# Transposed output tiles of a gated mix: one DMA transpose per tile, narrower store pieces, one store semaphore

## The chip, the cores and the metric

The kernel runs on one core of a Trainium2 chip. The metric is the device time of one execution in microseconds. Ratios are the mean time of one kernel's runs over the mean of the runs of the kernel before in the same rounds; they are therefore not quite the ratio of the medians that are quoted beside them.

Names: PE is the matrix engine, DVE the vector engine, ACT the scalar engine, POOL the general engine (here, after a few small set-up operations, it only issues four loads), SP the engine whose queue issues nearly all DMAs, "SPq" in the profile. PEld is the loading of weights into PE.

## The reference, cut to what matters

```python
x = A_x                                        # 1 x 2048 x 640, bf16
g = sigmoid((x * gate_w).sum(-1, keepdims=True))
a = ssm(x)                                     # complex diagonal state space, 640 states, scan over 2048 steps
b = gelu(x @ w1 + b1) @ w2 + b2                # 640 -> 1728 -> 640
return g * a + (1 - g) * b
```

## The kernel before

The 2048 rows of x are handled as four tiles (`q` = 0 to 3) of 512 rows. Tiles 0 to 2 are computed transposed, with features on the partitions (`xT[q]`: 128 partitions x 5 feature blocks x 512 rows). DVE adds the parts of the result into `xT[q]`. Five DMA transposes, one for each feature block, then bring the tile back into row order, into a buffer `xn`, and one DMA stores it. Tile 3 is computed in row order chunk by chunk at the end and needs no transpose.

```python
xn = [SB(f"xn_{i}", [128, 4, D], BF16) for i in range(2)]        # two buffers, D = 640
# ...
# in outsT(q), q = 0, 1, 2:
op(f"o{q}", "dve", d_dve(2560, 2), K1, XT[q], lambda: tt(xf, xf, e1, ALU.add), prio=P)
load_T(f"oT{q}", f"l_oT{q}", [(xn[q % 2][:, :, d * 128:(d + 1) * 128], xT[q][:, d, :]) for d in range(KD)],   # KD = 5
       [("xn", q % 2, 0), ("xn", q % 2, 1)], 402 + q, 5.0, reads=XT[q])

def f_st():
    return dma_inc("sp", nc.sync.dma_start(o2[q * 512:(q + 1) * 512, :].rearrange("(c p) d -> p c d", p=128), xn[q % 2][:, :, :]), f"sto{q}")

op(f"sto{q}", "sp", 0.5, [("xn", q % 2, 0), ("xn", q % 2, 1)], [], f_st, prio=403 + q, lat=3.0)
```

`xn` has a second use: it holds the rows of x from which the gate is computed. POOL loads x of tile 2 into the first buffer and x of tile 3 into the second, so each of these loads has to wait until the store of tile 0 or tile 1 has read the buffer. Behind the load of tile 3 comes a chain: the gate product on DVE, a tanh on ACT, two small operations on DVE.

```python
def xnload(q, eng, prio=None):          # q = 2 and 3 are issued by POOL
    load(f"xn{q}", eng, f"l_xn{q}", xn[q % 2][:, :, :],
         x2[q * 512:(q + 1) * 512, :].rearrange("(c p) d -> p c d", p=128),
         [("xn", q % 2, 0), ("xn", q % 2, 1)], prio, dur=1.0, lat=6.0)
```

A list scheduler in the file fixes the order of instructions on each engine at build time.

## Time and profile before

The kernel before takes 213.39 us (median of 3; 212.97 to 213.45). Its profiled execution spans 213.0 us.

| Reading of the kernel before | Value | Where it is read |
|---|---|---|
| PE busy | 209.4 us, 98% | page, part 1 |
| DVE busy | 190.2 us, 89% | page, part 1 |
| From the start of steady matmuls to the last DVE operation | 14.63 to 210.29 us | chain that ended last |
| SP time to issue a tile's five transposes | 7.38, 7.00, 6.83 us | timeline of SP |
| Store of a tile, issue to landing | 6.3, 3.2, 3.2 us (tiles 0, 1, 2) | instructions of the store's line |
| Issue of the loads that reuse the buffers | 107.32, 156.99 us | timeline of POOL |

The page, part 1 (busy us, share of the span, number of instructions), of the kernel before:

```profile
PE 209.4 (98%) x1102; PEld 104.9 (49%) x1102; DVE 190.2 (89%) x240; ACT 103.2 (48%) x177; POOL 4.2 (2%) x12
```

The busy share alone does not prove that PE is the limit, since matmuls are pipelined. The Trainium skill has a pace to compare with: "TensorE: Matmul & The Clock Gate", section "Wait — 56ns, not 53.3ns?", says that warm back-to-back matmuls start N / 2.4 GHz + about 2.5 ns apart, 215.7 ns for N = 512. The chain below shows 65 such matmuls in 14.03 us, 215.8 ns each. This agrees within 0.1 ns, so in its steady part PE has nothing left to give at this number of matmuls.

The chain that ended last is what the profile finds when it starts from the last instruction and goes back, at each step, to what released it. In order of time (start us, duration us, what), of the kernel before:

```profile
14.63 5.40 PE ps L653 x25
...
144.85 14.03 PE ps L653 x65
158.88 14.06 PE ps L920 x78
...
204.80 5.47 PE ps L832 x50
210.27 0.02 issue
210.29 0.35 DVE W1sb L866
```

Every piece left out between 14.63 and 210.27 us is PE as well. No transpose, store or load of the output path stands in this chain.

The timeline of SP (start us, duration us of the issue, line, operation, what, how many) of the kernel before. L340 is the transpose, L992 the store of a tile:

```profile
91.79 7.38 SPq L340 DMA_TRANSPOSE xn<-xT  x5
100.40 0.38 SPq L992 DMA_DIRECT2D out_dram<-xn  x1
...
144.97 7.00 SPq L340 DMA_TRANSPOSE xn<-xT  x5
153.21 0.38 SPq L992 DMA_DIRECT2D out_dram<-xn  x1
...
192.65 6.83 SPq L340 DMA_TRANSPOSE xn<-xT  x5
```

The timeline of POOL, with the idle time before each load and what ended it in brackets:

```profile
107.32 0.77 POOL L333 DMA_DIRECT2D xn<-in_A_x_dram  x1 [64.08 <-DMA out_dram<-xn]
156.99 0.75 POOL L333 DMA_DIRECT2D xn<-in_A_x_dram  x1 [48.90 <-DMA out_dram<-xn]
```

These 113 us of waiting are the longest entry in the list of waits; POOL has no other work. What matters is when the reader of the loaded rows runs. It is DVE line 606, from 125.89 us for tile 2 and from 168.39 us for tile 3, without any wait before it.

### The profile page before, as it was taken

To read this page: it belongs to the slowest core of one execution; us is meant where nothing else is said; L and a number is where in the kernel's file an instruction comes from. 1 tells how busy PE (TensorE), PEld (TensorE's weight loads), DVE (VectorE), ACT (ScalarE), POOL (GpSimd) and SP (SyncE) were. 2 spreads that over 40 slices of the span, in tenths; PEclk is the share of its full clock that TensorE was granted. 3 is DMA by queue.
4 is the path that set the end of the run, shared out by engine and by line. 5 is a ranking of instruction groups with operands and counts; after the bars stand their busy time and mean duration, and the time that the engine had idled before them with its cause. 6 is when DMAs were issued, how large, how long until landed. Compare 5 with 4: busy or idle time off the path is not lost.

```text
span 213.0 us, 2755 instructions
## 1 busy us (share of the span) xinstructions
PE 209.4 (98%) x1102; PEld 104.9 (49%) x1102; DVE 190.2 (89%) x240; ACT 103.2 (48%) x177; POOL 4.2 (2%) x12
## 2 busy tenths in 40 slices
PE   8999999999999999999999999999999999999994
PEld 3444444444564444444464444444456444567774
DVE  2399999999999999999999999899999999499734
ACT  2389556679860353556680073456660037523330
POOL 1000000210000000000010000000010000000000
DMA  6999999999400020043474000005542000002531
GB/s 169 274 259 176 190 184 299 288 140 224 100 0 3 0 49 0 0 51 75 123 46 120 9 0 0 0 2 77 117 140 87 0 3 0 0 0 58 148 105 63
DMA packets 42664, 19.08 MB, mean 90 GB/s; under 512 B 34076, under 2 KB 41372, under 8 KB 42652
## 3 DMA queue, kind: packets, MB, share of 16 engines
q1 hardware_dynamic: 40992, 17.59, 37.6%
q0 software_dynamic: 1600, 1.32, 4.4%
q8 instruction: 8, 0.13, 0.3%
q14 instruction: 4, 0.03, 0.1%
q10 hardware_dynamic: 60, 0.01, 0.1%
HBM read 8.41 MB, written 2.63 MB: 52 GB/s over the span
## 4 chain that ended last, share of the span: by engine, by line
PE 97%; DMA 1%; DVE 0%; issue 0%
PE ps L653 22%; PE ps L696 20%; PE ps L920 20%; PE ps L967 15%; PE ps L783 7%; PE ps L832 5%; PE ps L631 5%; DMA xn<-in_A_x_dram 1%; PE ps L674 1%; PE ps L931 1%; PE ps L419 1%; PE ps L797 0%; DVE W1sb L866 0%; PE ps L438 0%
## 5 line engine op out<-in xcount | busy, mean ns | idle before, releaser
L653 PE MATMUL ps<-xT,W1sb 128*128 128x512 bf16 x220 | 48.1, 379 | 0.0
L736 DVE TENSOR_TENSOR_SCAN W<-atab,V 128x1280 bf16<-128x1280 f32 x16 | 44.3, 2812 | 0.3
L696 PE MATMUL ps<-xT,BT 128*128 128x512 bf16 x200 | 43.8, 379 | 0.0
L920 PE MATMUL ps<-Gl,W2sb 128*128 128x512 bf16 (+1 forms) x234 | 42.7, 344 | 0.0
L660 ACT ACTIVATE Gl<-ps,cols 128x512 bf16<-128x512 f32 x44 | 29.9, 694 | 15.5 <-PE ps L653 15.5
L653 PEld LDWEIGHTS ps<-xT,W1sb 128*128 128x128 bf16 x220 | 21.5, 98 | 26.0
L967 PE MATMUL ps<-Hb,CT 128*128 128x512 bf16 x150 | 32.9, 379 | 0.0
L920 PEld LDWEIGHTS ps<-Gl,W2sb 128*128 128x128 bf16 x234 | 22.9, 98 | 19.3
L705 ACT ACTIVATE U<-ps 128x512 bf16<-128x512 f32 x40 | 23.7, 596 | 15.6 <-PE ps L696 15.6
L696 PEld LDWEIGHTS ps<-xT,BT 128*128 128x128 bf16 x200 | 19.5, 98 | 23.8 <-ACT Gt L682 0.4
L938 ACT ACTIVATE E1T<-ps,cols 128x512 bf16<-128x512 f32 (+1 forms) x18 | 9.5, 624 | 36.0 <-PE ps L931 36.0
L967 PEld LDWEIGHTS ps<-Hb,CT 128*128 128x128 bf16 x150 | 14.5, 98 | 17.9 <-DVE Hb L488 0.3
L975 ACT ACTIVATE E2T<-ps 128x512 bf16<-128x512 f32 x15 | 9.1, 604 | 13.6 <-PE ps L967 13.6
L783 PE MATMUL ps<-W2sb,Gl 128*128 128x320 bf16 x104 | 14.8, 299 | 0.0
L606 DVE SCALAR_TENSOR_TENSOR trf<-xn,gwb 128x640 bf16<-128x640 bf16 x16 | 13.2, 823 | 0.4
L488 DVE TENSOR_TENSOR Hb<-Hb,V 128x1280 bf16<-128x1280 bf16 x16 | 12.5, 821 | 0.3
L488 DVE TENSOR_TENSOR V<-V,W 128x1280 bf16<-128x1280 bf16 x16 | 12.5, 820 | 0.3
L488 DVE TENSOR_TENSOR V<-mr,U 128x2560 bf16<-128x2560 bf16 x8 | 11.9, 1492 | 0.3
L783 PEld LDWEIGHTS ps<-W2sb,Gl 128*128 128x128 bf16 x104 | 10.1, 98 | 4.3 <-issue 0.3
L488 DVE TENSOR_TENSOR Hb<-c,W 128x2560 bf16<-128x2560 bf16 x8 | 11.9, 1490 | 0.2
L488 DVE TENSOR_TENSOR W<-mi,U 128x2560 bf16<-128x2560 bf16 x8 | 11.9, 1483 | 0.0
L488 DVE TENSOR_TENSOR V<-s,W 128x2560 bf16<-128x2560 bf16 x8 | 11.9, 1483 | 0.0
(91 smaller groups left out, 151.7 us busy)
## 6 DMA issues: line engine op xcount, KB each, us to landing
W2sb<-in_B_w_dram SPq DMA_DIRECT2D x1, 2080.0 KB, 9.1
out_dram<-xn SPq DMA_DIRECT2D x3, 640.0 KB, 3.2
W1sb<-in_B_w_dram SPq DMA_DIRECT2D x5, 256.0 KB, 4.0
xn<-in_A_x_dram POOLq DMA_DIRECT2D x2, 640.0 KB, 7.0
trf<-grow SPq DMA_DIRECT2D x3, 256.0 KB, 4.8
xn<-in_A_x_dram SPq DMA_DIRECT2D x1, 640.0 KB, 7.3
W1sb<-in_B_w_dram SPq DMA_DIRECT2D x1, 480.0 KB, 5.2
out_dram<-W1sb SPq DMA_DIRECT2D x3, 160.0 KB, 1.8
```

The costliest lines, as they stand in the source:

```text
L488: return inc("dve", nc.vector.tensor_tensor(out=o, in0=a, in1=b, op=o_))
L606: t = inc("dve", nc.vector.scalar_tensor_tensor(out=scr[:, :], in0=xn[q % 2][:, c, :], scalar=1.0, in1=gwb[:, :], op0=ALU.mult, op1=ALU.mu ...
L631: return inc("pe", nc.tensor.matmul(PS[jf][:, t0:t1], W1sb[:, k, jf * 128:(jf + 1) * 128], xT[0][:, k, t0:t1], start=(k == 0 and t0 == 0), ...
L653: t = nc.tensor.matmul(PS[bank][:, :], W1sb[:, k, jf * 128:(jf + 1) * 128], xT[q][:, k, :], start=(k == 0), stop=(k == KD - 1))
L660: return inc("act", nc.scalar.activation(Gl[q % 2][:, jf, :], PS[bank][:, :], ACT.Gelu_apprx_tanh, bias=b1col[:, jf:jf + 1]))
L696: t = nc.tensor.matmul(PS[bank][:, :], BT[:, ci, kd, k * 128:(k + 1) * 128], xT[q][:, kd, :], start=(kd == 0), stop=(kd == KD - 1))
L705: return inc("act", nc.scalar.activation(dst, src, ACT.Copy, scale=1.0 if ci == 0 else -1.0))
L736: t = inc("dve", nc.vector.tensor_tensor_scan(out=g[:, ci, :], data0=a, data1=v[:, ci, :], initial=0.0, op0=ALU.mult, op1=ALU.add))
L783: t = nc.tensor.matmul(PS[bank][:, 0:HALF], Gl[q % 2][:, jf, t4 * 128:(t4 + 1) * 128], W2sb[:, jf, cols], start=False, stop=False, skip_gr ...
L832: t = nc.tensor.matmul(PS[bank][:, 0:n], H[b % NHB][:, ci, k, s * 128:(s + 1) * 128], CT[:, ci, k, cols], start=(i == 0), stop=(i == 2 * K ...
L920: t = nc.tensor.matmul(PS[bank][:, 0:t1 - t0], W2sb[:, jf, d * 128:(d + 1) * 128], Gl[q % 2][:, jf, t0:t1], start=(jf == 0), stop=False)
L967: t = nc.tensor.matmul(PS[bank][:, :].rearrange("p (s t) -> p s t", s=2), CT[:, ci, k, d * 128:(d + 1) * 128], Hb[:, 2 * (q % 2):2 * (q % ...
```

## The change

The intent is to free SP and shorten the output path: one transpose instruction handles all 20 blocks of a tile. The transpose instruction writes the blocks one after another in the order of its input (feature block, chunk), so the buffer is no longer in row order, and the store has to put it right: it writes pieces of 128 elements (256 B) instead of whole rows of 640 (1280 B). The three stores count on one semaphore instead of three.

```diff
-            load_T(f"oT{q}", f"l_oT{q}", [(xn[q % 2][:, :, d * 128:(d + 1) * 128], xT[q][:, d, :]) for d in range(KD)],
+            on = xn[q % 2][:, :, :].rearrange("p c d -> p (c d)")
+            load_T(f"oT{q}", f"l_oT{q}", [(on.rearrange("p (b r) -> p b r", r=128), xf)],
                    [("xn", q % 2, 0), ("xn", q % 2, 1)], 402 + q, 5.0, reads=XT[q])
 
             def f_st():
-                return dma_inc("sp", nc.sync.dma_start(o2[q * 512:(q + 1) * 512, :].rearrange("(c p) d -> p c d", p=128), xn[q % 2][:, :, :]), f"sto{q}")
+                return dma_inc("sp", nc.sync.dma_start(o2[q * 512:(q + 1) * 512, :].rearrange("(c p) (d r) -> p d c r", p=128, r=128),
+                                                        on.rearrange("p (d c r) -> p d c r", d=KD, r=128)), "sto")
 ...
-        for q in range(NQ - 1):
-            nc.sync.wait_ge(sems[f"sto{q}"], E.count[f"sto{q}"])
+        nc.sync.wait_ge(sems["sto"], E.count["sto"])
```

## The prediction

> **What bounds the kernel now.** The matrix engine. The page gives PE busy 209.4 of 213.0 us (98%) at a granted clock of 1.0, and the chain of waits that ended last is 97% PE: from 3.8 us to 210.3 us it is matmul after matmul with no DMA piece in it. After that only the last vector operation (0.35 us) and the final 32 KB store (2.3 us to landing) remain. PE waits for others well under 1 us after the start.
>
> **What the change touches.** The order of instructions is the same on PE, DVE and ACT; POOL's differs only in line numbers and the semaphore it waits on. On the SP queue, three groups of five transposes become three single ones (128x20x128), and each 640 KB store is cut into 256 B pieces instead of 1280 B (2560 pieces instead of 512).
>
> Transposes: five issues of 4 blocks cost 7.38, 7.00 and 6.83 us of SP time (timeline of SP), about 8.4 us from first issue to the store's issue. The existing loads of xT with 20 blocks in one instruction took a median of 3.4 us to issue and 5.4 us to land, though from DRAM. I expect 3.5 us (3 to 5) and 5 to 6.5 us to landing: SP gets about 3.5 us back per tile, the store is issued 2 to 3 us earlier.
>
> Store: it landed in 3.2 us (once 6.3). The Trainium skill, "DMA: Bandwidth & Descriptors", section Specifications, says that pieces under 512 B cost a read-modify-write. This trace has no comparable store. From the queue table (hardware queue: 40992 packets, 37.6% of 16 engines' span) a packet took about 31 ns on average; 2560 of them over 16 engines give an estimate of 5 us, plus about 1.5 us of start and receipt: 5 to 7 us. So transpose plus store stay near 12 us in total, within 3 us either way.
>
> **How much is on the critical path: none.** The stores release two loads of xn by POOL. The first load was issued at 107.3 us, takes 7 us, and its first reader (gate product on DVE) runs at 125.9: 11 us of slack. The second is issued at 157.0, lands about 164, and is read at 168.4: 4.4 us of slack, and behind that DVE idles 1.4 us (for ACT gth) and 1.3 us (for E2T) before 185.2, so about 7 us in all before PE could feel it. The third store is issued at 200.7 and would have to last beyond 210 to disturb the final stores. The row store of gates behind the first tile store may get slower (it took 13 us), but the broadcast it feeds is needed 18 us after it lands. The shared semaphore saves at most a wait or two that are already satisfied at the end.
>
> **Predicted time:** 213.3 us, range 212.6 to 214.2 (8 in 10). Faster by over 2%: 0.01; within 2%: 0.97; slower by over 2%: 0.02.
>
> **What would show each step.** Chain of waits still 97% PE with the same pieces; SP timeline with one transpose of 3 to 5 us per tile; issue list with the out store landing in 5 to 7 us; about 6100 more packets under 512 B (three times 2560, less 1536 of larger ones); POOL's second load issued within 3 us of 157.0; the end from the last matmul still 2.7 us.
>
> **What would make it wrong.** The 256 B store far slower than estimated (above 10 us), so that the gate product at 168.4 is late by more than the DVE slack, or so that the third store is still draining under the last two; or a single SBUF-to-SBUF transpose much slower than five, through back-pressure. Either would show as DVE waiting for the xn load, or a longer end after the last matmul.

## The result, and the profile after

The changed kernel takes 213.39 us (median of 6; 213.11 to 214.09), the kernel before 213.42 us in the same comparison (median of 6; 212.94 to 213.85). The ratio is 1.0004, with a 95% interval from 0.9983 to 1.0025. The change does not move the time.

The chain that ended last, of the changed kernel:

```profile
13.98 5.39 PE ps L653 x25
...
144.20 14.03 PE ps L653 x65
158.23 14.06 PE ps L920 x78
...
204.15 5.47 PE ps L832 x50
209.62 0.03 issue
209.65 0.35 DVE W1sb L866
```

The profiled execution of the changed kernel spans 212.2 us, 0.8 us less than that of the kernel before, and the chain shows that this is no gain. From the start of the steady matmuls to the last DVE operation, the kernel before took 210.29 - 14.63 = 195.66 us and the changed one 209.65 - 13.98 = 195.67 us. Most of the 0.8 us (14.63 - 13.98 = 0.65) lies before 15 us, where both kernels run the same instructions and the first loads land a little earlier or later from one execution to the next.

What was changed did change. The timelines of SP and of POOL in the changed kernel (L993 is the store of a tile):

```profile
91.15 2.95 SPq L340 DMA_TRANSPOSE xn<-xT  x1
97.57 0.70 SPq L993 DMA_DIRECT2D out_dram<-xn  x1
...
142.49 4.46 SPq L340 DMA_TRANSPOSE xn<-xT  x1
150.44 0.65 SPq L993 DMA_DIRECT2D out_dram<-xn  x1
...
192.00 3.71 SPq L340 DMA_TRANSPOSE xn<-xT  x1
```

```profile
104.90 0.77 POOL L333 DMA_DIRECT2D xn<-in_A_x_dram  x1 [62.40 <-DMA out_dram<-xn]
155.78 0.75 POOL L333 DMA_DIRECT2D xn<-in_A_x_dram  x1 [50.11 <-DMA out_dram<-xn]
```

SP spends 2.95 to 4.46 us on a tile's transposes instead of 6.83 to 7.38. The store's issue costs 0.65 us instead of 0.38, and the store lands in 4.8 us (median) instead of 3.2. The loads by POOL are issued 2.4 and 1.2 us earlier, part of which is the earlier start of this execution. The readers of those loads, DVE line 606, run at the same place in the DVE order as before (from 167.73 us for tile 3), without a wait. The gain ends there.

The packets tell the same. The page, part 2, of the kernel before and then of the changed one:

```profile
DMA packets 42664, 19.08 MB, mean 90 GB/s; under 512 B 34076, under 2 KB 41372, under 8 KB 42652
```

```profile
DMA packets 48424, 19.08 MB, mean 90 GB/s; under 512 B 41372, under 2 KB 47132, under 8 KB 48412
```

The difference in total is 5760. Three stores of 2560 instead of 512 pieces add 6144, and 12 transposes fewer take away 384, which is 32 each. The two runs that do half of the change each confirm both terms (below: 48808 and 42280 packets, 6144 more and 384 fewer than before).

### The profile page after: what moved, and what is told of

Its sections match the earlier page's. It is cut to its first block, busy times and chain, and to the rows that moved or that the text cites. A ratio compares the mean times of both kernels' runs of the same rounds, so it can differ in the third digit from the quotient of the medians.

```text
span 212.2 us, 2742 instructions
## 1 busy us (share of the span) xinstructions
PE 208.4 (98%) x1102; PEld 104.4 (49%) x1102; DVE 190.1 (90%) x240; ACT 103.2 (49%) x177; POOL 4.2 (2%) x12
## 4 chain that ended last, share of the span: by engine, by line
PE 94%; SPq 2%; DMA 2%; issue 0%; DVE 0%
PE ps L653 22%; PE ps L696 20%; PE ps L920 20%; PE ps L967 15%; PE ps L783 7%; PE ps L832 5%; DMA W1sb<-in_B_w_dram 2%; PE ps L631 2%; SPq L340 1%; PE ps L674 1%; SPq L333 1%; PE ps L931 1%; PE ps L797 0%; DVE W1sb L866 0%
## 5 line engine op out<-in xcount | busy, mean ns | idle before, releaser
L660 ACT ACTIVATE Gl<-ps,cols 128x512 bf16<-128x512 f32 x44 | 29.8, 693 | 15.5 <-PE ps L653 15.5
```

The lines of the kernel that those rows point to most:

```text
L660: return inc("act", nc.scalar.activation(Gl[q % 2][:, jf, :], PS[bank][:, :], ACT.Gelu_apprx_tanh, bias=b1col[:, jf:jf + 1]))
```

## The experiments

My theory: PE is the limit throughout, and the whole path from an output tile to its store, and on through the reused buffer, has so much slack that neither the gain nor the cost of the change reaches PE. The rival: the path does matter, and the faster transpose and the slower store cancelled. A second question is how large the slack is, because a claim of "off the critical path" is worth little without its size.

### No transposes at all

This takes away the whole of what the change tries to shorten. The output is wrong (a relative error of 1.22).

```diff
-            load_T(f"oT{q}", f"l_oT{q}", [(on.rearrange("p (b r) -> p b r", r=128), xf)], ...)
 ...
-                return dma_inc("sp", nc.sync.dma_start(... on.rearrange("p (d c r) -> p d c r", d=KD, r=128)), "sto")
+                return dma_inc("sp", nc.sync.dma_start(... xT[q][:, :, :], as it lies, in rows of 640 ...), "sto")
```

> The changed kernel without any transpose of output tiles: each tile is stored as it lies, so the output is wrong on purpose. Theory (the whole path from output tile to store is off the critical path): time as before, ratio 1.000 within 0.3%, although the store of each tile is issued about 6 us earlier. Rival (the path matters, and the faster transpose and the slower store cancelled): with all the transpose time gone the kernel is faster by 1 us or more, ratio at most 0.995.

Measured: 213.45 us (median of 6), kernel before 213.61 us (median of 11), ratio 0.9987 (0.995 to 1.0023). The loads by POOL were issued at 94.19 and 148.75 us, 13.1 and 8.2 us earlier than in the kernel before, and nothing came of it. The rival's 0.995 stands just at the edge of the interval, so the times alone do not exclude a gain of up to 0.5%. The chain that ended last of this run is closer:

```profile
13.44 5.40 PE ps L653 x25
...
209.11 0.35 DVE W1sb L866
```

From the start of the steady matmuls to the last DVE operation it takes 209.11 - 13.44 = 195.67 us, as in the two kernels above, and the same 195.67 us stand in the profiles of the next three runs. With every transpose of output tiles gone, the stretch is the same within 0.01 us, so these transposes do not set it, and a gain on them has nothing to cancel.

### Five transposes with the narrow store

```diff
-            load_T(f"oT{q}", f"l_oT{q}", [(on.rearrange("p (b r) -> p b r", r=128), xf)],
+            load_T(f"oT{q}", f"l_oT{q}", [(on[:, d * 512:(d + 1) * 512].rearrange("p (b r) -> p b r", r=128), xT[q][:, d, :]) for d in range(KD)],
```

> Five transposes per tile as before, the store in 256 B pieces as in the changed kernel. Theory: ratio 1.000 within 0.3%; SP again spends about 7 us issuing a tile's transposes, about 8 us from first issue to the store's issue, and the store still lands in 4.8 us. So the second load of x is issued about 158.5 us, later than in both kernels, and nobody waits for it. Rival (cancelling): slower than before by the store's 1.6 us or more.

Measured: 213.24 us (median of 4), kernel before 213.61 us, ratio 0.9973 (0.9922 to 1.0024). It is the cost of the change without its gain, and it is not slower. SP again spent 7.36, 6.79 and 7.23 us on the transposes, and the store landed in 4.8 us (median). The load of tile 3 was issued at 156.03 us, not at 158.5: in this execution, as in the changed kernel's, the transposes of tile 1 began at 142.6 us, not at 144.97. That expectation missed because I had taken the start from the kernel before. The start depends on a small DMA ahead of it in SP's order, discussed at the end.

### One transpose with the wide store

The transpose writes its blocks in input order. If the last DVE addition writes its result in (chunk, feature block) order, into the buffer `E2T`, which is free by then, the single transpose gives row order and the store can keep its 1280 B pieces.

```diff
-            op(f"o{q}", "dve", d_dve(2560, 2), K1, XT[q], lambda: tt(xf, xf, e1, ALU.add), prio=P)
+            yf = E2T[:, :, :].rearrange("p d t -> p (d t)")
+            op(f"o{q}", "dve", d_dve(2560, 2), K1 + XT[q], K2,
+               lambda: tt(yf.rearrange("p (c d r) -> p d c r", d=KD, r=128), <xT[q] as (d, c, r)>, <E1T as (d, c, r)>, ALU.add), prio=P)
 ...
-            load_T(... [(on.rearrange("p (b r) -> p b r", r=128), xf)], ... reads=XT[q])
+            load_T(... [(on.rearrange("p (b r) -> p b r", r=128), yf)], ... reads=K2)
 ...  (and the store of the kernel before, on the shared semaphore)
```

> One transpose per tile and the store in 1280 B pieces again: the last addition on the tile writes its result in chunk-major order into a buffer that is free by then, so that one transpose gives the row order. Theory: ratio 1.000 within 0.3%; SP spends 3 to 4.5 us per tile on the transpose, the store lands in 3.2 us (two of three), the addition stays at about 1.5 us. Rival (cancelling): the gain without the cost, so faster than before by 1.5 us or more.

Measured: correct, 213.14 us (median of 6), ratio 0.998 (0.9938 to 1.0023). It is the gain without the cost, and it is not faster by anything that these runs resolve. The addition with permuted output took 1.49 us, as before; SP spent 2.96, 3.70 and 3.58 us per transpose; the store landed in 3.2 to 5.4 us, median 3.5. I do not call this version better than the other three.

The four kernels form a two by two table. For tile 0, the time from the first transpose's issue to the issue of POOL's load (from the timelines of SP and POOL) is:

| Tile 0, us | store in 1280 B pieces | store in 256 B pieces |
|---|---|---|
| five transposes | 107.32 - 91.79 = 15.5 | 107.81 - 91.13 = 16.7 |
| one transpose | 103.52 - 91.14 = 12.4 | 104.90 - 91.15 = 13.8 |

One transpose saves about 3 us, the narrow pieces cost about 1.3 us, and the two add up. For tile 1 they do not: 12.0, 13.4, 9.2 and 13.3 us in the same order. There the single transpose took 5.4 us from its issue to the store's issue with the wide store (144.99 to 150.38) and 7.95 us with the narrow one (142.49 to 150.44), although the instructions differ only in the source buffer; the second also began 2.5 us earlier. I have not found out why.

### A semaphore for each store again

```diff
-                ... on.rearrange("p (d c r) -> p d c r", d=KD, r=128)), "sto")
+                ... on.rearrange("p (d c r) -> p d c r", d=KD, r=128)), f"sto{q}")
```

> The changed kernel with one semaphore for each store, as before the change. Theory: ratio 1.000 within 0.3% and the same times of every store; the shared semaphore takes away only waits that are long satisfied at the end. Rival: if the shared count lets a load start too early or too late, the issue times of the two later loads of x differ from 104.9 and 155.8 us by more than the 1 us of the start's jitter.

Measured: 213.73 us (median of 4), ratio 1.0001 (0.9959 to 1.0043). The loads were issued at 106.01 and 156.25 us, 1.1 and 0.5 us later than in the changed kernel's profile; the first is 0.1 us beyond the 1 us that I had allowed. The store of tile 0 itself was issued 0.35 us later in this execution. The rest is jitter: from the issue of that store to the issue of the load it took 8.1 us here (97.92 to 106.01), and in the seven profiles with the shared semaphore and the same transpose and store of tile 0 (the changed kernel and the six runs below) 7.3 to 8.1 us. The Trainium skill, "DMA: Bandwidth & Descriptors", section "Why a DMA increments its semaphore by 16 and not by 1", warns that with two DMAs in flight on one semaphore a wait can pass before the first has landed. The trace shows that no two tile stores are ever in flight together: they are issued at 97.57, 150.44 and 199.34 us and land within 6.8 us. The sharing is harmless here because of that distance, not by construction.

### How much slack: delaying the store of tile 1

The changed kernel, with n more stores of tile 1 into scratch memory ahead of the real one. They count on the same semaphore, so POOL's load of tile 3 waits for all of them and stays free of races.

```diff
+        spare = nc.dram_tensor("spare", [n, 512, D], BF16, kind="Internal").ap()
 ...
             def f_st():
+                for i in range(n if q == 1 else 0):
+                    dma_inc("sp", nc.sync.dma_start(spare[i].rearrange("(c p) (d r) -> p d c r", p=128, r=128),
+                                                        on.rearrange("p (d c r) -> p d c r", d=KD, r=128)), "sto")
```

With n = 3:

> The changed kernel with three more stores of the second tile, into scratch, ahead of the real one; the load that reuses the buffer waits for all four. Estimate from the changed kernel: each store in 256 B pieces drains for about 3.1 us, so the load is issued about 9 us later than 155.8, near 165, and lands near 172. Two readings of the slack: the one in my prediction (7 us before PE feels it) gives 2 us slower, near 215.5; the one that also counts the DVE's slack behind (4.9 us to the gate product, 2.8 us of DVE idle before 184.5, 6.2 us until the last two projections need their states: 13.9 us) gives no change, ratio 1.000 within 0.3%.

Measured: 213.81 us (median of 4; 213.27 to 215.67), kernel before 213.18 us, ratio 1.0045 (0.9996 to 1.0093). The load was issued at 165.28 us. This execution ran 0.08 us ahead of the changed kernel's, so the load was 9.6 us late (the texts written before the later runs say 9.4). DVE did wait for it, which neither kernel does:

```profile
170.07 0.82 DVE L607 SCALAR_TENSOR_TENSOR trf<-xn,gwb 128x640 bf16<-128x640 bf16 x1 [2.33 <-DMA xn<-in_A_x_dram]
```

PE, in the list of waits, waited for nothing new, and its last piece began at 204.07 us (204.15 in the changed kernel). The prediction's 7 us of slack falls with this profile, but one of the four runs was 2 us slow. (Single runs like it also occur in the kernel before: 215.78 and 215.93 us, one among eleven in each of two comparisons.)

> The kernel with three extra stores of the second tile once more, with more rounds, since one of its four runs was 2 us slower and left the ratio at 1.0045 with an interval from 0.9996 to 1.0093. If its delay of 9.4 us is absorbed, as its profile says (PE's waits unchanged): ratio 1.000 within 0.3%. If a part reaches PE: 1.003 or more again.

Measured: 213.52 us (median of 6), kernel before 213.41 us (median of 11), ratio 0.9992 (0.9948 to 1.0035). The load was issued at 165.90 us, late by about as much. The delay of 9.6 us is absorbed; the slow run did not return.

With n = 6:

> As the run with three, but six more stores of the second tile: the load is issued about 18.6 us late, near 174. Reading with 13.9 us of slack: about 4.7 us slower, near 218, with PE waiting for DVE before the projection of the last two chunks. Reading with 7 us: 11 to 12 us slower, near 225. Rival theory that the output path has no bearing at all: still 213.4.

Measured: 218.25 us (median of 4), kernel before 213.18 us, ratio 1.0224 (1.019 to 1.0258), so about 4.8 us slower. The size is as the larger reading of the slack expected. As to the place, I had named the projection of the last two chunks, waiting for states from DVE. The list of waits of this run shows another place before it. These are the lines that matter here (engine, line, what it waited for: us in total, times, longest us; the added code moves the line numbers, so the gate product is L607 here):

```profile
DVE trf L607 <- DMA xn<-in_A_x_dram: 13.2, 1, 13.2
ACT W1sb L812 <- DVE g1col L619: 9.4, 1, 9.4
PE ps L833 <- ACT W1sb L812: 3.9, 1, 3.9
PEld ps L833 <- DVE Hb L489: 0.4, 1, 0.4
```

Only the last line, 0.4 us, is the wait that I had named. The line above it came first: PE needs a PSUM bank for the projection of tile 3's first chunk; ACT has yet to evict that bank; the eviction is scaled by the gate; and the gate columns stand on DVE behind the late gate product and a whole scan. Following the delay down that chain, each time against the changed kernel moved by 0.32 us (the later start of this execution), shows where the 20.3 us went:

| Step | Changed kernel + 0.32, us | n = 6, us | Later by, us |
|---|---|---|---|
| POOL issues the load of tile 3 | 156.10 | 176.45 | 20.3 |
| DVE starts the gate product | 168.05 | 181.31 | 13.3 |
| DVE has started the last gate column operation | 183.34 | 195.05 | 11.7 |
| ACT starts the eviction | 188.38 | 195.31 | 6.9 |
| PE starts the projection of the first chunk | 191.81 | 195.89 | 4.1 |

Each hand-over had some slack of its own: 7.1 us because the load is early, 1.5 us where DVE used to wait for ACT, 4.8 us where ACT used to wait for PE, 2.9 us where PE did not need the bank yet. Together they are about 16 us.

The 0.4 us understate the wait that I had named, because PE comes to it late already. The chain that ended last in this run does not pass through the bank at all. From the gate product on, it stays on DVE to the end:

```profile
189.54 5.54 DVE W L737 x2
...
207.02 1.56 DVE Hb L489 x2
...
213.65 1.13 DVE W1sb L867 x3
```

The states `Hb` were complete at 208.58 us. PE started their projection, its last piece of work, at 208.64 us, 4.3 us later than the changed kernel moved by 0.32 us (203.99 + 0.32 = 204.31). So without the wait for the bank, PE would have lost about the same here (an inference from this trace, not a run of its own). The slack on this path is 7.1 and 1.5 us as above, 1.4 us where DVE used to wait for `E2T`, and 6.0 us between the states' completion (197.97 us in the changed kernel) and PE's need of them: about 16 us too. Two hand-overs to PE gave way at nearly the same delay.

With n = 5, to see whether that is a fixed amount:

> Five extra stores of the second tile. With three the load was 9.4 us late, with six 20.3 us, so with five about 16.7 us (an estimate). With six, PE lost 4.1 us at the first projection of the last tile and 4.3 to 4.7 us in all, so about 15.9 us were absorbed there; with five PE should lose about 0.8 us, ratio about 1.004, at the same place: ACT's eviction of the first chunk, which waits for the gate scale from DVE. If the absorption is not a fixed amount but a share of the delay: about 3.9 us slower, ratio 1.018.

Measured: 213.8 us (median of 6), kernel before 213.41 us, ratio 1.0011 (0.9971 to 1.0051). The load was issued at 172.02 us; this execution ran 0.43 us ahead of the changed kernel's, so it was 16.7 us late. The list of waits shows PE just touched, at both places (again the lines that matter):

```profile
DVE trf L607 <- DMA xn<-in_A_x_dram: 9.5, 1, 9.5
ACT W1sb L812 <- DVE g1col L619: 6.4, 1, 6.4
PEld ps L833 <- ACT W1sb L812: 0.6, 1, 0.6
PE ps L833 <- ACT W1sb L812: 0.3, 1, 0.3
PEld ps L833 <- DVE Hb L489: 0.4, 1, 0.4
```

PE's last projection started at 204.23 us, 0.7 us later than in the changed kernel moved by 0.43 us; between the medians there are 0.4 us, which the interval does not tell from none. The slack is a fixed amount, close to 16 us: 9.6 us late is free, 16.7 us costs less than 1 us, 20.3 us costs 4.8. The 1.018 of the other reading is far outside the interval.

### The end of the kernel: delaying the store of tile 2

The same edit for `q == 2`, whose store is issued near the end.

> The changed kernel with one more store of the third tile, into scratch, ahead of the real one, near the kernel's end. The real one then lands about 3.1 us later, near 207.5, before the last two stores are issued at 209.6 to 210.4. Expected: ratio 1.000 within 0.3%.

Measured with one extra store: 213.25 us (median of 4), ratio 1.0009 (0.9989 to 1.0028). Free, as expected.

> As the run with one, but three more stores of the third tile. Four stores of about 3.1 us from 200 on drain until about 213, and the last stores queue behind them: about 2 to 3.5 us slower, 215.5 to 217, with the matmuls ending where they did and a longer time from the last matmul to the end (2.6 us in the changed kernel, 5 or more here). If the last stores overtake the queue instead: 213.4.

Measured with three: 216.28 us (median of 4), ratio 1.0145 (1.013 to 1.016), about 3.1 us slower, as expected. The timeline of SP in this run shows the form of it (L995 the extra stores, L997 the real one, L890 and L876 the stores of tile 3's chunks):

```profile
199.27 6.07 SPq L995 DMA_DIRECT2D spare<-xn  x3
205.38 3.01 SPq L997 DMA_DIRECT2D out_dram<-xn  x1
208.43 3.74 SPq L890 DMA_DIRECT2D out_dram<-W1sb  x2
212.21 0.95 SPq L876 DMA_DIRECT2D out_dram<-W1sb  x2
```

In the changed kernel the last line of this timeline reads:

```profile
209.60 0.81 SPq L875 DMA_DIRECT2D out_dram<-W1sb  x2
```

The matmuls end at the same time as ever (the chain's last piece starts at 204.06 us for 5.47 us), but the last two stores are issued 2.6 us later, because SP itself is held: a store that costs 0.65 us of SP time in an empty queue costs 3.0 us once others are ahead of it. From the last matmul to the end it takes 5.4 us instead of 2.6. So at the end of the kernel the same path has only a few microseconds of slack: one extra store is free, three are not.

## Why the prediction was right

- **The limit.** Right. PE's pace of 215.8 ns per matmul of 512 columns is the same before and after, and the stretch from 14 us to the last DVE operation is 195.66 and 195.67 us. The share of PE in the chain that ended last did fall, from the 97% that I had said would stay to 94%. The whole of that is at the start: in the changed kernel's execution the chain passes through the first issues on SP and one load of w1 instead of through the first matmuls.
- **The transpose.** Issue: 3 to 5 us expected, 2.95 to 4.46 measured. From issue to the store's issue: 5 to 6.5 us expected, 6.4 us for tile 0 and 7.95 us for tile 1 measured (tile 2's transpose landed in 5.2 us). So the second was too low for tile 1, and the store came 0.3 us earlier relative to the transposes' start there, not 2 to 3 (for tile 0 it was 2.2). POOL's second load came at 155.78 us, within the 3 us allowed around 157.0.
- **The store.** 5 to 7 us expected, 4.8 us measured (6.8 for tile 0). The estimate from the mean packet time was a little high. The Trainium skill, "DMA: Bandwidth & Descriptors", section Specifications, says that pieces under 512 B cost a read-modify-write. The trace agrees that they cost: 1.2 to 1.6 us per 640 KB. It does not show by what mechanism.
- **The packets.** About 6100 more "under 512 B" were expected; 7296 more were measured under 512 B and 5760 more in total. I had put the difference of the total (2560 less 512, three times) against the wrong class, and had left out the 32 packets that each DMA saved takes with it.
- **The critical path: none.** Right, and the experiments show it in both directions: without any transposes the stretch is the same within 0.01 us, and with the load of tile 3 9.6 us late nothing is lost.
- **The size of the slack.** Wrong, though on the safe side: "about 7 us in all" is about 16 us. Two terms failed. First, I took 7 us for the load's time to landing, the median of two loads. By themselves they took 9.2 us (tile 2) and 4.7 us (tile 3), so the load of tile 3 is early by 6.7 us (7.1 us in the changed kernel), not 4.4. Second, my sum stopped at DVE. It left out that PE does not need the states until 6.0 us after DVE has them, and that on the way over the bank ACT and then PE have slack of their own (4.8 and 2.9 us). The two waits of DVE that I did count, 1.4 and 1.3 us, are both on the path of the states; only the first is on the way over the bank.
- **The end.** 2.7 us from the last matmul expected to stay, 2.6 measured; a third store that drains too long does disturb the last ones, as the prediction's last paragraph said, once it is lengthened by about 9 us.

## What to carry to other kernels

Before shortening a path, delete it once, even with wrong output: if the time stays, and the stretch that sets it stays in the profile too, no cleverness on that path can pay. To know how safe it is to lengthen a path, delay it by known amounts until the time moves, and then read in the list of waits which hand-over gave way first; it may not be the one that you expected. Read the chain that ended last as well: a wait that comes later can look small only because an earlier one has already made the engine late. Slack adds up over the hand-overs of a chain, and it shrinks towards the end of the kernel, where a late store delays the last ones through the queue that they share.

## What the Trainium skill lacked or had wrong

- "DMA: Bandwidth & Descriptors", section "Issuing engines are not separate DMA queues", says that the sequencer's time to initiate a DMA is usually small relative to the DMA itself. Here one transpose of a 640 KB tile held SP for 2.95 to 4.46 us of the 6.4 to 7.95 us until its store was issued, five smaller ones for about 7 of 8.4 us, and a 640 KB store in 256 B pieces for 3.0 us when three like it were ahead, against 0.65 us with none. A DMA that waits behind others can hold up its issuing engine.
- The same page has no measured time on trn2 of a store in 256 B pieces from the hardware queue. Here 640 KB in 256 B pieces landed in 4.8 us against 3.2 us in 1280 B pieces (medians), and six such stores in a row delayed what followed by 20.3 us, 3.4 us each.
- No page has a time for a store of single elements. In the kernel before, 2 KB written to memory as 512 pieces of 4 B (`grow<-gcol`) took 10.5 us (median of three), longer than any 640 KB store of that run (3.2 to 6.3 us). The next DMA but one on SP, the transposes of tile 1, started at 142.5 or at 145.0 us, according to how long this took: for that tile 8.7 us in the changed kernel, 10.5 us in the kernel before, 11.2 us in the run with one transpose and the wide store. What decides it was not found.
